# A four-layer fp32 transformer stack on one NeuronCore: a re-dealt beginning, sums held in PSUM, moved reciprocals and later weight pieces

## The chip, the cores and the metric

The kernel runs on one core of one Trainium2 chip. The metric is the device time of one execution in microseconds (us), here the median of several runs. A second kernel, the changed one, is compared with it run by run. The engines are named as the profile names them: PE is TensorE's matrix multiply, PEld its weight load, DVE is VectorE, ACT is ScalarE, POOL is GpSimd, and SP is SyncE, whose queue issues most DMA transfers. On-chip results of PE go to PSUM, which has eight banks; everything else is in SBUF.

## The reference

Four layers A, B, A, B with residual sums run over one sequence of 2048 tokens with 512 features, 32 heads of 16. Cut to what matters:

```python
def _A_ref(x, wqkv, w_phi, wo):              # 16 features per head, dual softmax
    q, k, v = split_heads(x @ wqkv)
    pq, pk = q @ w_phi, k @ w_phi            # per head
    phi_q = concat([softmax(pq), softmax(-pq)])
    phi_k = concat([softmax(pk), softmax(-pk)])
    kv, z = sum_s(phi_k * v), sum_s(phi_k)
    o = (phi_q @ kv) / (phi_q @ z + 1e-6)
    return o @ wo

def _B_ref(x, wq, wk, wv, wo, beta):         # 4 segments of 512 tokens
    for s in range(4):
        p = softmax(qs @ ks.T * 16 ** -0.5 + causal_mask)
        a_dot = p @ vs
        a_mem = (phi(qs) @ M) / (phi(qs) @ z + 1e-6)     # phi(t) = t + 1 or exp(t)
        o = g * a_mem + (1 - g) * a_dot                  # g = sigmoid(beta)
        M, z = M + phi(ks).T @ vs, z + sum(phi(ks))
    return o @ wo

x = x + A(layernorm(x)); x = x + B(layernorm(x))
x = x + A(layernorm(x)); x = x + B(layernorm(x))
```

The mask adds -1e9 where the query's index is below the key's, so a query here sees the keys up to its own. Inputs and output are float32, 2048 by 512.

## The kernel before

**Tiles.** A tile is 128 tokens by 512 features; a segment is four tiles (512 tokens). A product that must keep float32 accuracy is made from three products in the faster fp32r format: each operand is split into a high part (`hi`, a cast on ACT) and a low part (`lo`, the operand minus its high part, on DVE or POOL), and hi x hi, hi x lo and lo x hi are added in one PSUM bank. `mm3` issues these three for each of the four blocks of 128 input features (`kc` 0 to 3). PSUM is shared out as three banks named `g` for products of all kinds, one `pv`, one `mx`, one `my` and one pair `lg`.

**Order.** Every engine works its own instructions off in program order and waits by semaphores. The order in which the program issues them is written by hand. Several generators (projections of the next segment, output products of the last, weight pieces, layernorms) are advanced by tables of step names and numbers: a table entry says at which step which generator moves by how many pieces. So a table that changes shifts instructions on all engines at once.

**Layer A, first pass.** `LayerA.first` opens the program: `WARM` idle matmuls on zeros, then the transfers in the order of the string `ARRIVE` (x0 to x3 are the first four token tiles; k0, k1, v0, v1, q0, q1 the halves of the weights; `ident`, `bd`, `phi` small constants on ACT's queue), then the steps of the string `BEGINNING`. Its letters: m is a tile's statistics, g and r the root for a pair of tiles, n the normalisation, c the transposes of a tile with its split (`columns`), V, K, Q the split of one block of a weight matrix (a `p` behind it puts the low part on POOL), k and q a step of the fold, which multiplies phi into the key or query weights (transposes of the raw weights, then `phibd` matmuls), v a step of the value projection, u a step of the next segment's layernorm, p the spreading of phi. Later `pass1` projects all segments and sums the key-value products into `kva`. Near its end it fetches the output weights `awo`, high and low part of four blocks, eight pieces of 256 KB. They are advanced one piece at a step while t is 5 and 7 in a loop over the last eight projections. A transfer of that group is paced: it waits for the newest PE instruction at its place in the program.

**Layer A, second pass**, makes the numerators (the `KN` matmuls), divides, and multiplies by `awo` (`w` with `oh`, `ol`).

**Layer B** runs 32 half-head groups of four segments, each in five steps. In a step PE makes score products into `mx` and `my`, whose row maxima DVE takes (the custom instruction of the profile, with its accumulator `mxs`), then scores into `lg`, exponentials on ACT (`P`), the causal cut on POOL and the products with v into `pv`. The tables `GAPS` (segments before the last), `LAST`, `FINAL` (the last segment of the first and of the last layer B) and `BEFORE` say which filler moves in which step. When a pair of half-head groups is done, its denominators go through DRAM: `compact` loads them as `dn`, `flip` inverts them on DVE, `put` stores them, `load` fetches them spread over the heads into `KN` and `mmq`, and then `scaled`, `scaled_old` and `joined` use them on POOL. The offsets of these steps stand in `INVERT` and `JOIN`; the middle entry is for the two middle segments, the last for the last segment. Each is due so many steps after the group.

**The end of a layer B** (`close_last`) is written out in the string `TAIL`. There, p is the next piece of `early`, which multiplies the first three blocks of each of the last four token tiles by the output weights; P is all that is left of it; o transposes a tile of the last head group and divides it; t turns a tile back by a transpose, adds the memory's part and splits the sum; a multiplies the fourth block, adds the result to the tile `xe` (named `tb` in the profile) and stores it. `early` itself adds its partial sums to `xe` on DVE. In the first layer B steps of the next layer's projections stand between these; in the last layer nothing does.

The helpers through which all matmuls, transposes and other instructions are issued are lines 198, 202 and 176 of the profile, so groups are told apart by tile names.

Of the kernel before, what the change touches and what calls it, by code (L numbers as in the profile page):

```python
# [32 lines left out]
G = 3  # L33
# [77 lines left out]
3.0 x1 | 3.1 max | 3.3 pre out/2 | 3.4 out/2  # L111
4.1 max out/1~ | 4.3 pre out/3 x2 | 4.4 a3 out/1
5.1 max out/2 x3 | 5.3 fin out/2~ | 5.4 pre
6.1 max | 6.3 fin
7.1 pt p/2 | 7.3 p/4 fin | 7.4 p/3
"""
BEFORE = {-25: "q0 load", -23: "v0", -21: "k0", -18: "n", -17: "v1 n", -16: "n", -15: "n n", -14: "q1 n", -13: "n", -12: "k1 n", -11: "n", -10: "v2 n", -4: "max q2~", -1: "t0"}


@with_exitstack  # L120
def interleave_kernel(ctx, tc, x_in, a_wqkv, a_wphi, a_wo, b_wq, b_wk, b_wv, b_wo, b_beta,
# [504 lines left out]
    class LayerA:  # L626
# [88 lines left out]
        def pass1(self, first):  # L715
# [35 lines left out]
            for n, s in enumerate(SEGS):  # L751
# [121 lines left out]
                for t in range(8):  # L873
                    for n, _ in enumerate(kproj(t, e) if t < 4 else qproj(t - 4, e, later)):
                        if t == 7 and n == SEAM:
                            if QFIRST:
                                scale_q(e[5])
                            begun(2)
                            self.e.update({4 * s + t: e[4 + t] for t in range(3)})
                            seam()  # L880
                            self.second = self.pass2()
                            for _ in range(AHEAD):
                                next(self.second)
                        if t in (5, 7):
                            next(weights, None)
                        yield
# [114 lines left out]
    class LayerB:  # L1001
        def __init__(self, xsrc, xdst, cut, final):
            self.xsrc, self.xdst, self.cut, self.final = xsrc, xdst, cut, final
            self.st, self.hT, self.vv, self.ot, self.mx, self.U = {}, {}, {}, {}, {}, {}
            self.pr, self.pv, self.pk, self.num, self.old, self.oT = {}, {}, {}, {}, {}, {}
            self.dens, self.inv = {}, {}
            self.later, self.late, self.rows, self.xq = [], [], [], []
# [346 lines left out]
        def close_last(self, rest):  # L1354
# [16 lines left out]
            def turned(t):  # L1371
# [4 lines left out]
                act.copy(hi[:, cut], old[:, cut])  # L1376
                dve.tensor_tensor(out=lo[:, cut], in0=old[:, cut], in1=hi[:, cut].bitcast(F32), op=SUB)

            def added(t):
                po = PS("g", G)  # L1380
                for _ in self.product(po, s, t, range(NC - 1, NC)):
                    pass
                dve.tensor_tensor(out=self.xe[t], in0=po, in1=self.xe[t], op=ADD)
                sync.dma_start(out=self.xdst[4 * s + t], in_=self.xe[t])
# [9 lines left out]

        def product(self, po, s, t, kcs):
            yield from mm3(po, lambda a, kc: self.oT[s, kc][a][:, t * P : (t + 1) * P],
                           lambda b, kc: self.wo[b][:, kc, :], kcs)

# [17 lines left out]
        def early(self):  # L1416
# [229 lines left out]
```

## Time and profile before

| | us |
|---|---|
| median of 3 runs | 1425.59 |
| smallest and largest run | 1425.07 and 1429.27 |
| profiled execution, its own time | 1427.28 |
| span of the profiled execution | 1425.5 |
| PE busy in it | 1374.1 |
| DVE busy | 956.1 |
| ACT busy | 810.5 |
| POOL busy | 731.9 |
| HBM read and written | 115.54 MB and 41.55 MB |

How to read it: the span runs from the first to the last recorded instruction, and the profiled execution's own time is 1.8 us longer. A row of the timeline gives the start, the busy time, the engine, the line and operation, the tiles out<-in, the count, and in brackets the idle time before it on that engine with what ended it. A row of the windows gives the stretch, its length, the busy time of PE, PEld, DVE, ACT and POOL (with counts), the granted clock of PE as a share of full speed, the DMA engines' share and GB/s. A row of the waits gives who waited for whom: total us, times, and the longest. "issue" stands where an instruction waited for nothing that the profile shows.

### The profile page before, as it was taken

Reading aid. Unit: us, or ns where it says so; the run is one execution under the profiler, and the core shown is the slowest. Engines: PE = TensorE matmul, PEld = TensorE weight load, DVE = VectorE, ACT = ScalarE, POOL = GpSimd, SP = SyncE. Lnnn points to the kernel's source line nnn. Section 1 sums busy time; section 2 is a strip of 40 time slices with the busy share of each in tenths; the row PEclk is TensorE's granted clock in tenths of the full one; section 3 lists DMA queues with packets and bytes.
Section 4 is the critical chain, followed back from the end, with each engine's and each line's share of the span. In section 5 each row is a group of like instructions: output and inputs, shape, how many; then the busy total and the mean of one; then the engine's idle time right before and its main releaser. Section 6 shows DMA issues by size and latency. Waiting matters only on the chain.

```text
span 1425.5 us, 33178 instructions
## 1 busy us (share of the span) xinstructions
PE 1374.1 (96%) x12070; PEld 946.6 (66%) x12070; DVE 956.1 (67%) x3038; ACT 810.5 (57%) x1246; POOL 731.9 (51%) x1067
## 2 busy tenths in 40 slices
PE   9999999999999999999999999999999999999987
PEld 7787778765666565655568887886656565556544
DVE  5766788677667556667556768958776755666673
ACT  5555345447676566556544434553666755765654
POOL 1678765324565556544524446641455555654543
PEclk9999999999999999999999999999999999999999
DMA  5369275636655646556630104854465566555551
GB/s 196 119 226 335 93 253 174 188 112 181 185 138 159 174 119 176 153 164 188 195 132 33 60 31 132 269 179 142 127 185 151 140 182 159 143 162 145 141 141 68
DMA packets 134898, 222.72 MB, mean 156 GB/s; under 512 B 26032, under 2 KB 39472, under 8 KB 134736
## 3 DMA queue, kind: packets, MB, share of 16 engines
q1 hardware_dynamic: 132768, 219.96, 51.9%
q8 instruction: 97, 1.59, 0.5%
q10 hardware_dynamic: 1968, 0.64, 0.2%
q14 instruction: 65, 0.53, 0.1%
HBM read 115.54 MB, written 41.55 MB: 110 GB/s over the span
## 4 chain that ended last, share of the span: by engine, by line
PE 74%; DVE 8%; ACT 7%; DMA 4%; POOL 3%; issue 3%; SPq 1%; ACTq 0%; POOLq 0%; DVEq 0%
PE g L198 45%; PE pv L198 8%; PE lg L198 8%; PE mx L198 4%; PE g L202 3%; PE my L198 3%; ACT P L176 3%; POOL P L176 1%; PE lg L202 1%; DVE es L176 1%; DVE my L176 1%; DVE mx L176 1%; SPq L176 1%; DMA e<-ta 1%; DVE junk L176 1%
## 5 line engine op out<-in xcount | busy, mean ns | idle before, releaser
L176 ACT ACTIVATE P<-lg 128x1024 f32<-128x1024 f32 x316 | 325.0, 1028 | 176.2 <-PE lg L198 160.1
L176 POOL TENSOR_SCALAR_AFFINE_SELECT P<-P 128x256 f32<-128x256 f32 (+1 forms) x448 | 190.5, 440 | 406.7 <-ACT P L176 404.6
L176 DVE CUSTOM_DVE_ANT_0 junk<-mx,mask 128x128 uint8<-128x128 f32 (+2 forms) x384 | 147.3, 421 | 125.4 <-PE my L198 87.7
L198 PE MATMUL g<-hh,wqk 128*128 128x512 f32 x512 | 185.1, 410 | 0.7 <-ACT mt L176 0.7
L198 PE MATMUL lg<-e,e 64*128 64x512 f32 (+1 forms) x1010 | 166.1, 386 | 14.7 <-ACT P L176 13.7
L198 PE MATMUL g<-w,oh 128*128 128x512 f32 x512 | 171.0, 415 | 2.0 <-ACT oh L176 1.5
L198 PE MATMUL pv<-P,v 128*32 128x512 f32 (+3 forms) x2048 | 164.8, 439 | 5.3 <-ACT ot L176 5.3
L176 DVE CUSTOM_DVE_ANT_0 mx<-mx,mask 128x512 f32<-128x512 f32 x128 | 89.0, 695 | 107.1 <-PE my L198 84.7
L198 PEld LDWEIGHTS lg<-e,e 64*128 64x128 f32 x1010 | 80.0, 184 | 112.0 <-issue 50.4
L198 PE MATMUL my<-e,e 63*128 63x256 f32 (+3 forms) x519 | 147.8, 345 | 5.4 <-DVE mxs L176 4.2
L198 PE MATMUL mx<-e,e 63*128 63x256 f32 (+3 forms) x519 | 147.8, 336 | 0.8 <-DVE mxs L176 0.5
L176 DVE CUSTOM_DVE_ANT_0 junk<-my,mask 128x128 uint8<-128x128 f32 (+2 forms) x384 | 146.7, 419 | 0.0
L198 PE MATMUL g<-w,hh 128*128 128x512 f32 x448 | 143.8, 402 | 0.3 <-ACT hh L176 0.3
L198 PEld LDWEIGHTS pv<-P,v 128*32 128x32 f32 x2048 | 53.7, 109 | 106.9 <-issue 93.3
L198 PEld LDWEIGHTS g<-hh,wqk 128*128 128x128 f32 x512 | 96.2, 188 | 32.2 <-issue 11.8
L198 PEld LDWEIGHTS g<-w,oh 128*128 128x128 f32 x512 | 88.3, 189 | 32.5 <-issue 13.2
L198 PE MATMUL g<-w,ol 128*128 128x512 f32 x256 | 101.8, 398 | 3.7 <-DVE ol L176 3.1
L198 PE MATMUL g<-hl,wqk 128*128 128x512 f32 x256 | 100.3, 392 | 0.0
L176 DVE DVE_READ_ACCUMULATOR2_ANT mxs<- 128x1 f32 x1024 | 100.1, 98 | 0.0
L198 PEld LDWEIGHTS mx<-e,e 63*128 63x128 f32 (+1 forms) x519 | 90.5, 185 | 10.1 <-DVE mxs L176 4.2
L198 PEld LDWEIGHTS my<-e,e 63*128 63x128 f32 (+1 forms) x519 | 83.8, 185 | 17.7 <-DVE mxs L176 10.6
L198 PEld LDWEIGHTS g<-w,hh 128*128 128x128 f32 x448 | 80.3, 188 | 22.8 <-issue 6.3
(183 smaller groups left out, 2834.8 us busy)
## 6 DMA issues: line engine op xcount, KB each, us to landing
e<-ta SPq DMA_DIRECT2D x384, 128.0 KB
wqk<-wqk SPq DMA_DIRECT2D x64, 512.0 KB
x<-x SPq DMA_DIRECT2D x48, 256.0 KB
xr<-x SPq DMA_DIRECT2D x32, 256.0 KB
x<-xr SPq DMA_DIRECT2D x28, 256.0 KB
tmp<-U SPq DMA_DIRECT2D x56, 128.0 KB
KN<-inv SPq DMA_DIRECT2D x28, 256.0 KB
pq<-tb SPq DMA_DIRECT2D x24, 256.0 KB
```

Of the source, the lines that this page charges most:

```text
L176: i = f(*a, **k)
L198: return held(nc.tensor.matmul(*a, **k))
L202: return held(nc.tensor.transpose(*a))
```

## The change

It has six parts. (1) `ARRIVE`, `BEGINNING` and `WARM`: the key weights arrive ahead of the value weights and x2, x3 behind them, the fold of phi into the key weights runs ahead of the first token tile, tiles 2 and 3 get their statistics ahead of three low parts, and 12 idle matmuls take the place of 18. (2) `INVERT` and `JOIN`: for middle segments `flip` moves from offset 4.5 to 5.0 and `scaled_old` from 10.5 to 10.0; for the last segment `scaled` moves from 10.5 to 9.5. (3) The end of a layer B: `HELD` keeps the sums of tiles 2 and 3 in their PSUM bank, so that `added` goes on in it and `early` adds nothing on DVE; `BYPV` puts tile 1's last product in the `pv` bank; `LOWS` puts the low parts of tiles 0 to 2 on POOL; `TAIL` is written anew. `BYACT` is empty, so its branch is not used. (4) `AWO`: while t is 5 only two weight pieces are advanced in place of one at each step. (5) `UPC` moves one step from 14 to 13, which leaves every engine's order as it was. (6) Entries of `GAPS`, `LAST`, `FINAL` and `BEFORE` move by a step or a place.

```diff
-INVERT = (((2.5, 4.5, 5, 7), (2.5, 4.5, 5, 7), (2.5, 4.5, 5, 7), (2.5, 4.5, 5, 7)), ((2.5, 4.5, 5, 7), (2.5, 4.5, 5, 7), (2.5, 4.5, 5, 7), (2.5, 4.5, 5, 7)), ((2.5, 4.5, 5.5, 7.5), (2.5, 4.5, 5.5, 7.5), (2.5, 4.5, 5.5, 7.5), (2.5, 4.5, 5.5, 7.5)))
+INVERT = (((2.5, 4.5, 5, 7), (2.5, 4.5, 5, 7), (2.5, 4.5, 5, 7), (2.5, 4.5, 5, 7)), ((2.5, 5.0, 5, 7), (2.5, 5.0, 5, 7), (2.5, 5.0, 5, 7), (2.5, 5.0, 5, 7)), ((2.5, 4.5, 5.5, 7.5), (2.5, 4.5, 5.5, 7.5), (2.5, 4.5, 5.5, 7.5), (2.5, 4.5, 5.5, 7.5)))
...
-JOIN = (((9.5, None, None, 11, 12.5), (9.5, None, None, 11, 12.5), (9.5, None, None, 11, 12.5), (9.5, None, None, 11, 12.5)), ((9.5, 10.5, 11.5, 12, 13.5), (9.5, 10.5, 11.5, 12, 13.5), (9.5, 10.5, 11.5, 12, 13.5), (9.5, 10.5, 11.5, 12, 13.5)), ((10.5, 11.5, 12.5, 13, 13.5), (10.5, 11.5, 12.5, 13, 13.5), (10.5, 11.5, 12.5, 13, 13.5), (10.5, 11.5, 12.5, 13, 13.5)))
+JOIN = (((9.5, None, None, 11, 12.5), (9.5, None, None, 11, 12.5), (9.5, None, None, 11, 12.5), (9.5, None, None, 11, 12.5)), ((9.5, 10.0, 11.5, 12, 13.5), (9.5, 10.0, 11.5, 12, 13.5), (9.5, 10.0, 11.5, 12, 13.5), (9.5, 10.0, 11.5, 12, 13.5)), ((9.5, 11.5, 12.5, 13, 13.5), (9.5, 11.5, 12.5, 13, 13.5), (9.5, 11.5, 12.5, 13, 13.5), (9.5, 11.5, 12.5, 13, 13.5)))
...
-WARM = 18
+WARM = 12
 FEW = 2
-ARRIVE = "x0 ident x1 v0 bd v1 x2 x3 phi k0 k1 q0 q1"
+ARRIVE = "x0 x1 ident k0 bd phi k1 v0 v1 x2 x3 q0 q1"
 BEGINNING = """
-m0 m1 g0 r0 n0 V0 n1a V1p c0 V2 V3p c1 m2 m3 v1 v1 v1 v1 g1 r1 p n2 k k v1 n3a v1 v1 v1 c2 k k c3 u k v1 v1 v1 K0 K1 K2 K3 v1 u u q q u q u v1 q v1 v1 u u u q Q0 Q2 v1 Q1 u Q3 u u
+m0 m1 g0 r0 k k n0 n1a k c0 c1 k p V0 k V1p V2p m2 m3 g1 v1 r1 V3p v1 v1 n2 n3a v1 K0 c2 K1 K3 K2 v1 v1 c3 v1 u v1 v1 v1 q v1 q v1 u u u q u v1 q v1 v1 u u u v1 q Q0 Q2 u Q1 Q3 u u
 """
-TAIL = "p o0 p o1 o2 p p t0 p o3 p t1 t2 P a0 a1 t3 a2 a3"
+TAIL = "p o0 p o1 o2 t0 p p p p o3 t2 P t1 a0 t3 a1 a2 a3"
...
+BYPV = (1,)
+HELD = (2, 3)
+BYACT = ()
+LOWS = (0, 1, 2)
...
-UPC = (2, 3, 4, 5, 11, 12, 13, 14, 15)
+UPC = (2, 3, 4, 5, 11, 12, 13, 13, 15)
+AWO = 2
...
-6.1 k1+/3~ max | 6.2 m3 n | 6.3 out/3 | 6.4 a0+ out/1 v1+/2
-7.0 n | 7.1 max v1+/2 q2+/1 begin | 7.2 n | 7.3 q2+/3~ n N | 7.4 t0+ v2+/4 N
+6.1 k1+/3~ max | 6.2 m3 | 6.3 out/3 | 6.4 a0+ out/1 v1+/2
+7.0 n n | 7.1 max v1+/2 q2+/1 begin | 7.2 n | 7.3 q2+/3~ n N | 7.4 t0+ v2+/4 N
...
-2.1 max out/2 | 2.3 out/1 | 2.4 a2 x0 pre
+2.1 max out/1 | 2.3 out/2 | 2.4 a2 x0 pre
...
-4.1 max out/1~ | 4.3 pre out/3 x2 | 4.4 a3 out/1
-5.1 max out/2 x3 | 5.3 fin out/2~ | 5.4 pre
+4.1 max out/1~ | 4.3 pre out/2 x2 | 4.4 a3 out/2
+5.1 max out/2 x3 | 5.3 fin out/2 | 5.4 pre
...
-BEFORE = {-25: "q0 load", -23: "v0", -21: "k0", -18: "n", -17: "v1 n", -16: "n", -15: "n n", -14: "q1 n", -13: "n", -12: "k1 n", -11: "n", -10: "v2 n", -4: "max q2~", -1: "t0"}
+BEFORE = {-25: "q0 load", -23: "v0", -21: "k0", -18: "n", -17: "v1 n", -16: "n", -15: "n n", -14: "q1 n", -13: "n", -12: "k1 n n", -10: "v2 n", -4: "max q2~", -1: "t0"}
...
-    def mm3(po, lhs, rhs, kcs=range(NC)):
+    def mm3(po, lhs, rhs, kcs=range(NC), first=True, last=True):
 
         for kc in kcs:
             for n, (a, b) in enumerate(((0, 0), (0, 1), (1, 0))):
-                mm(po, lhsT=lhs(a, kc), rhs=rhs(b, kc), start=(kc == kcs[0] and n == 0),
-                   stop=(kc == kcs[-1] and n == 2))
+                mm(po, lhsT=lhs(a, kc), rhs=rhs(b, kc), start=(first and kc == kcs[0] and n == 0),
+                   stop=(last and kc == kcs[-1] and n == 2))
...
-                        if t in (5, 7):
+                        if t == 7 or t == 5 and n < AWO:
                             next(weights, None)
...
-                dve.tensor_tensor(out=lo[:, cut], in0=old[:, cut], in1=hi[:, cut].bitcast(F32), op=SUB)
+                (pool if t in LOWS else dve).tensor_tensor(out=lo[:, cut], in0=old[:, cut], in1=hi[:, cut].bitcast(F32), op=SUB)
 
             def added(t):
-                po = PS("g", G)
-                for _ in self.product(po, s, t, range(NC - 1, NC)):
+                held = self.held.pop(t, None)
+                po = held or (PS("pv", PV) if t in BYPV else PS("g", G))
+                for _ in self.product(po, s, t, range(NC - 1, NC), first=held is None):
                     pass
...
             for t in range(4):
                 po = PS("g", G)
+                if t in HELD:
+                    self.held[t] = po
+                    yield from self.product(po, s, t, EARLY, last=False)
+                    yield
+                    continue
                 yield from self.product(po, s, t, EARLY)
```

Three places show what this does to the order of instructions. The first is PE at the very start, before (`x` are token tiles, `w` the value weights' parts, `hh` and `hl` the parts of the transposed tokens):

```order
L198 MATMUL pv_147<-oh_145 128x512 x18
L202 MATMUL g_215<-ident,x_134 128x128 x4
L202 MATMUL g_226<-ident,x_135 128x128 x4
L198 MATMUL g_242<-w_182,hh_180 128x512
L198 MATMUL g_242<-w_183,hh_180 128x512
L198 MATMUL g_242<-w_182,hl_181 128x512
```

and in the change (`P` are the raw key weights, `e` their transposes):

```order
L203 MATMUL pv_147<-oh_145 128x512 x12
L207 MATMUL g_204<-ident,P_5_138 128x128 x4
L207 MATMUL g_210<-ident,P_5_138 128x128 x4
L207 MATMUL g_218<-ident,P_6_139 128x128 x4
L207 MATMUL g_224<-ident,x_134 128x128 x4
L207 MATMUL g_231<-ident,x_135 128x128 x4
L207 MATMUL g_238<-ident,P_6_139 128x128 x4
L203 MATMUL lg_250<-phibd,e_31_203 128x128 x8
L203 MATMUL mx_251<-phibd,e_31_203 128x128 x4
L203 MATMUL my_252<-phibd,e_31_203 128x128 x4
L203 MATMUL g_285<-w_176,hh_174 128x512
```

The key weights' transposes and the fold stand ahead of the first value product, where the token tiles' transposes and two tiles of value products stood.

The second is DVE in the middle segments of a layer B, before (ISA is the custom maximum and the reading of its accumulator; `dn` the denominators):

```order
L176 TENSOR_TENSOR hl_5787<-g_5894,hh_5786 128x4x128
L176 RECIPROCAL dn_5840<-dn_5840 128x64
L176 ISA mx_5915,mxs_5878<-mx_5915,mask 128x512
L176 ISA mxs_5878 128x1
L176 ISA my_5916,mxs_5878<-my_5916,mask 128x512
L176 TENSOR_TENSOR xr_5837<-g_5708,xr_5837 128x512
```

and in the change:

```order
L181 TENSOR_TENSOR hl_5781<-g_5888,hh_5780 128x4x128
L181 ISA mx_5908,mxs_5872<-mx_5908,mask 128x512
L181 ISA mxs_5872 128x1
L181 ISA my_5909,mxs_5872<-my_5909,mask 128x512
L181 RECIPROCAL dn_5834<-dn_5834 128x64
L181 TENSOR_TENSOR xr_5831<-g_5702,xr_5831 128x512
```

The reciprocal is behind the pair of maxima; it is so in sixteen places.

The third is DVE in the last rows of the last layer B, before (`tb` are the result tiles, `ot` the turned tiles, `ol` their low parts):

```order
L176 RECIPROCAL r_18381<-my_18351 128x4
L176 TENSOR_TENSOR tmp_18308<-my_18351,r_18381 128x64
L176 TENSOR_TENSOR ot_17957<-lg_18352,ot_17957 128x128
L176 TENSOR_TENSOR ol_18349<-ot_17957,oh_18348 128x128
L176 TENSOR_TENSOR tb_3509_17623<-g_18392,tb_3509_17623 128x512
L176 TENSOR_TENSOR tb_3547_17772<-g_18398,tb_3547_17772 128x512
L176 TENSOR_TENSOR ot_17957<-lg_18352,ot_17957 128x128
L176 TENSOR_TENSOR ol_18349<-ot_17957,oh_18348 128x128
L176 TENSOR_TENSOR tb_3579_17918<-g_18408,tb_3579_17918 128x512
L176 TENSOR_TENSOR tb_3626_18114<-g_18414,tb_3626_18114 128x512
```

and in the change:

```order
L181 RECIPROCAL r_18369<-my_18340 128x4
L181 TENSOR_TENSOR tmp_18298<-my_18340,r_18369 128x64
L181 TENSOR_TENSOR ot_17944<-lg_18341,ot_17944 128x128 x2
L181 TENSOR_TENSOR tb_3507_17613<-g_18380,tb_3507_17613 128x512
L181 TENSOR_TENSOR ot_17944<-lg_18341,ot_17944 128x128
L181 TENSOR_TENSOR ol_18338<-ot_17944,oh_18337 128x128
L181 TENSOR_TENSOR tb_3545_17762<-pv_18390,tb_3545_17762 128x512
L181 TENSOR_TENSOR tb_3577_17908<-g_18318,tb_3577_17908 128x512
L181 TENSOR_TENSOR tb_3624_18104<-g_18342,tb_3624_18104 128x512
```

One result add instead of two stands ahead of the last turned tile, and the low parts of the other three tiles are on POOL.

More of the change, by code (lines that the diff above doesn't have):

```diff
@@ L1005, in __init__ @@
             self.pr, self.pv, self.pk, self.num, self.old, self.oT = {}, {}, {}, {}, {}, {}
-            self.dens, self.inv = {}, {}
+            self.dens, self.inv, self.held = {}, {}, {}
             self.later, self.late, self.rows, self.xq = [], [], [], []
@@ L1376, in turned @@
                 act.copy(hi[:, cut], old[:, cut])
-                dve.tensor_tensor(out=lo[:, cut], in0=old[:, cut], in1=hi[:, cut].bitcast(F32), op=SUB)
+                (pool if t in LOWS else dve).tensor_tensor(out=lo[:, cut], in0=old[:, cut], in1=hi[:, cut].bitcast(F32), op=SUB)
             def added(t):
-                po = PS("g", G)
-                for _ in self.product(po, s, t, range(NC - 1, NC)):
-                    pass
-                dve.tensor_tensor(out=self.xe[t], in0=po, in1=self.xe[t], op=ADD)
+                held = self.held.pop(t, None)
+                po = held or (PS("pv", PV) if t in BYPV else PS("g", G))
+                for _ in self.product(po, s, t, range(NC - 1, NC), first=held is None):
+                    pass
+                if t in BYACT:
+                    mid = T2("tb3", 2)
+                    act.copy(mid, po)
+                    pool.tensor_tensor(out=self.xe[t], in0=mid, in1=self.xe[t], op=ADD)
+                else:
+                    dve.tensor_tensor(out=self.xe[t], in0=po, in1=self.xe[t], op=ADD)
                 sync.dma_start(out=self.xdst[4 * s + t], in_=self.xe[t])
@@ L1393, in close_last, with product @@
                     dict(o=own, t=turned, a=added)[what[0]](int(what[1]))
-        def product(self, po, s, t, kcs):
+        def product(self, po, s, t, kcs, first=True, last=True):
             yield from mm3(po, lambda a, kc: self.oT[s, kc][a][:, t * P : (t + 1) * P],
-                           lambda b, kc: self.wo[b][:, kc, :], kcs)
+                           lambda b, kc: self.wo[b][:, kc, :], kcs, first, last)
         def ask(self, s, t):
```

## The prediction, made before the changed kernel ran

> **What bounds the kernel now.** I read the page first, busy shares and then the chain that ended last, and after it the waits of PE alone, since the page leaves little doubt about the engine:
>
> ```profile
> PE 1374.1 (96%) x12070; PEld 946.6 (66%) x12070; DVE 956.1 (67%) x3038; ACT 810.5 (57%) x1246; POOL 731.9 (51%) x1067
> PE 74%; DVE 8%; ACT 7%; DMA 4%; POOL 3%; issue 3%; SPq 1%; ACTq 0%; POOLq 0%; DVEq 0%
> PE lg L198 <- ACT P L176: 13.7, 25, 1.1
> PE my L198 <- DVE mxs L176: 4.2, 18, 0.3
> PE my L198 <- issue: 2.1, 1, 2.1
> PE lg L202 <- DVE ot L176: 2.0, 3, 0.9
> ```
>
> PE is busy for 1374.1 of 1425.5 us, so only 51.4 us of idle PE time are there to be won, in many small pieces. The last four rows are groups of such pieces: total us, times, longest. The change does not take work from PE except idle matmuls at the very start, so each part can win only what it removes of these pieces. The three short chains without matmul cover, namely the beginning and the two ends of a layer B, I read instruction by instruction. All else I price by the PE gap that disappears.
>
> **Later weight pieces (first layer A, about 170 us).** The largest single gap is the one put down to "issue":
>
> ```profile
> 169.13 1.15 PE L198 MATMUL my<-P,v 128*32 128x32 f32 x110
> 172.42 0.38 PE L198 MATMUL my<-P,v 128*32 128x32 f32 x18 [2.15 <-issue]
> 178.40 1.17 PE L198 MATMUL g<-KN,P 128*64 128x68 f32 x32
> 869.15 1.29 PE L198 MATMUL my<-P,v 128*32 128x32 f32 x128
> 876.14 1.17 PE L198 MATMUL g<-KN,P 128*64 128x68 f32 x32
> 164.44 2.39 SPq L176 DMA_DIRECT2D w<-awo  x4
> q8 instruction: 1, 0.02, 15.5%
> 172.00:174.00 2.00, 1.58 (x22) 1.29 (x23) 1.57 (x5) 1.09 (x2) 1.13 (x2) 0.76 0.00 0
> 174.00:176.00 2.00, 2.00 (x8) 1.61 (x7) 0.58 (x2) 0.00 (x0) 2.00 (x2) 0.50 0.37 86
> ```
>
> PE stops in the midst of a run of 128 equal matmuls, with no data to wait for. The one instruction packet stands in the traffic view of 170.0 to 170.4 us, just behind the four `awo` pieces issued from 164.44 on; the same stretch of the second layer A runs without a stop. From the start of the run to the first `KN` matmul it takes 9.27 us here and 6.99 us there, so the stop and its clock cost 2.28 us. The clock is in the windows (first number after POOL's): 0.76, then 0.50. My reading: PE's next block of instructions queued behind 1 MB of weights. The change lets only two pieces go at that place, so the packet comes through some 3 us sooner and the boundary passes unseen: **-2.3**, bounds -2.3 and 0. The two last pieces of the weights are then issued late, and must be there before the fourth block of the first output tile (the second row below):
>
> ```profile
> 174.16 4.69 SPq L176 DMA_DIRECT2D w<-awo  x4
> 185.80 0.40 PE L198 MATMUL g<-w,oh 128*128 128x512 f32 x1
> 221.66 6.15 DMA xr<-in
> ```
>
> The last of them is issued near 178.85 now and some 0.9 us later in the change (one more issue of the four that take 4.69 us). It has about 6.0 us; the slowest landing of a 256 KB piece among the long pieces of the chain is 6.15 us, so at worst it is a little late. I cost it at nothing and keep +1 for two layers in the range.
>
> The Trainium skill, "Runtime: NRT & Kernel Launch", section "Instruction fetch mechanics", says instructions are refilled in 16 KiB blocks and that a crossing is mostly hidden by the issue rate; by it the stop would have another cause, the move of the weights would win nothing, and the sum would be 2.3 us smaller. The trace has one such packet of 0.02 MB right before a 2.15 us stop, so I give that rule the smaller chance.
>
> **The reciprocal behind the maxima (both layers B).** `flip` of the middle segments moves behind one pair of 512-wide maxima, sixteen times. It pays where VectorE had the maxima waiting:
>
> ```profile
> 441.40 0.54 DVE L176 RECIPROCAL dn<-dn 128x64 f32<-128x64 f32 x1
> 442.45 0.73 DVE L176 CUSTOM_DVE_ANT_0 my<-my,mask 128x512 f32<-128x512 f32 x1
> 443.30 0.38 PE L198 MATMUL my<-e,e 63*128 63x256 f32 x1 [0.27 <-DVE mxs L176]
> 557.84 0.38 PE L198 MATMUL my<-e,e 63*128 63x256 f32 x1 [0.26 <-DVE mxs L176]
> 470.15 0.55 DVE L176 RECIPROCAL dn<-dn 128x64 f32<-128x64 f32 x1
> 471.18 0.70 DVE L176 CUSTOM_DVE_ANT_0 mx<-mx,mask 128x512 f32<-128x512 f32 x1 [0.48 <-PE my L198]
> ```
>
> At 441 the order on VectorE is reciprocal, mx, my, and the two matmuls that reuse those banks start late; without the reciprocal ahead they could start about 0.5 us sooner. The same picture stands at 557.84 and at its two counterparts in the last layer, four places in all. At 470, and at the other places, VectorE waits for PE after the reciprocal (0.48 us here), so nothing is won. 4 x 0.5 = **-2.0**; bounds 0 (another wait takes over each time) and -2.2. The neighbouring shifts of `JOIN` are on POOL with slack and cost nothing. The price of the move is one more hold on SP's queue, priced in the third rival.
>
> **The end of each layer B: held sums, `TAIL`, low parts on POOL.** Two of the four tiles no longer add twice: their sums of the early products stay in PSUM. That takes two adds and three low-part subtractions off VectorE in each end. In the last end nothing else runs, so VectorE's queue is the path:
>
> ```profile
> 1417.48 0.33 PE L202 MATMUL lg<-ident,tmp 128*128 128x128 f32 x1 [0.88 <-DVE ot L176]
> 1418.86 1.28 DVE L176 TENSOR_TENSOR tb<-g,tb 128x512 f32<-128x512 f32 x2
> 1420.06 0.28 DVE L176 TENSOR_TENSOR ot<-lg,ot 128x128 f32<-128x128 f32 x1
> 1420.72 0.73 PE L198 MATMUL g<-w,oh 128*128 128x512 f32 x2 [0.70 <-ACT oh L176]
> 1420.91 1.51 DVE L176 TENSOR_TENSOR tb<-g,tb 128x512 f32<-128x512 f32 x2
> 739.34 0.72 PE L198 MATMUL g<-w,oh 128*128 128x512 f32 x2 [0.79 <-ACT oh L176]
> ```
>
> Now the fourth tile's `ot` add at 1420.06 stands behind two result adds (1.28 us), and the last add ends at 1420.91 + 1.51 = 1422.42. In the new order one add (0.7) stands ahead of the fourth tile; each transposed tile also starts sooner, because neither a low part nor an early add is queued ahead on VectorE. By hand I get: first transposed tile ready near 1415.5, fourth tile's `ot` ready 1418.1, its low part 1418.8, the four result adds one after another from 1417.2 with the last at 1420.6: **-1.8**. POOL's 128-wide subtraction has no row; the rows of that form on VectorE take 0.28 and a 512-wide one on POOL 1.48 (row in the next part). With three in a line at 1.48 the third ends near 1420.5 and the gain shrinks to almost nothing; I take the near end, as the tile is a quarter as wide. Bounds -2.2 and 0.
>
> The first end, near 740 us, has matmuls of the next layer as cover, and gaps like the 0.79 at 739.34 are all there is: **-0.5**, bounds -1.2 and +0.3 (two of the three `g` banks are held, and one product waits for the third).
>
> **Beginning.** The key weights now arrive ahead of the value weights, the fold of phi into them runs first, and 12 idle matmuls stand where 18 did:
>
> ```profile
> 1.36 6.45 PE L198 MATMUL pv<-oh 128*128 128x512 f32 x18 [1.36 <-POOL oh L176]
> 1.70 5.57 DMA P<-in
> 7.28 0.62 ACT L176 CAST w<-P 128x512 fp32r<-128x512 f32 x1 [1.06 <-DMA P<-in]
> 10.73 1.48 POOL L176 TENSOR_TENSOR w<-P,w 128x512 fp32r<-128x512 f32 x1 [0.23 <-ACT w L176]
> 18.30:22.30 4.00, 3.99 (x37) 3.99 (x37) 1.58 (x3) 1.79 (x4) 0.00 (x0) 1.00 0.61 190
> ```
>
> The third transfer lands at 7.27 whichever matrix it brings. PE then transposes two key blocks where it transposed x tiles at 8.05, so it starts some 0.8 us sooner; the fold that fills 18.8 to 22.5 moves to about 11 to 14.5. The first value product comes at 14.5 and waits about 0.5 us for POOL's low parts (1.48 each, and the third cannot start before ScalarE's third cast). From there the same matmuls follow. What is won at 7.3 is given back at the low parts and at one `g` bank: **0**, bounds -1.3 and +1.5. Twelve idle matmuls end near 1.36 + 12 x 0.36 = 5.7, with 1.6 us of silence after them; the stop at 170 shows that 2.15 us can halve the clock, which is inside the +1.5.
>
> The tables `GAPS`, `LAST`, `FINAL`, `BEFORE` shift output products by one or two places between neighbours that are PE work of the same kind; **0**, within 0.5 each way.
>
> **Sum.** -2.3 - 2.0 - 1.8 - 0.5 = -6.6 us. The profiled execution took 1427.28 us with a span of 1425.5 (1.8 around it), so it stands 1.7 above the median; the sum is a difference and I set it against the median: 1425.59 - 6.6 = **1419.0 us**. From one measurement to the next, 0.3% (4.3 us) is about what can be told from no change: below 1421.3 is faster, above 1429.9 slower.
>
> **Rivals.** First, *the stop stays*: the fetch still falls behind two weight pieces, or has another cause. Then -4.3, 1421.3, on the border. For it: 0.5 MB still goes ahead. Against: the second layer A. Second, *only the ends count*: the four maxima gaps are refilled by the next wait, PE <- ACT P being the largest group with 13.7 us. Then -2.3 - 1.2 (part of the tail) = -3.5, 1422.1; with the stop too, 1424.4: no change that can be told. Third, *SP is held longer*, the slower side:
>
> ```profile
> 442.35 0.55 SPq L176 DMA_DIRECT2D inv<-dn  x1
> 1335.26 0.44 SPq L176 DMA_DIRECT2D inv<-dn  x1
> 448.10 0.32 SPq L176 DMA_DIRECT2D wqk<-wqk  x1
> 615.11 5.22 DMA inv<-dn
> 628.25 0.56 PE L198 MATMUL lg<-e,e 64*128 64x256 f32 x4 [0.93 <-ACT P L176]
> ```
>
> `put` of the inverse can only go after the reciprocal; SP stands at it, and then at the load of its result, with six loads of the next scores behind. In the chain of waits the transfer at 615.11 takes 5.22 us and the scores behind it cost PE 0.93 at 628.25. Setting the new end of each reciprocal (after its maxima) against the old `put`, eleven of the sixteen (the first at 442.35, the last at 1335.26) are later, by 0.4 to 2.5 us, 19 us in sum. If half of that reaches PE, +9.7 stands against the -2.0: -6.6 + 2.0 + 9.7 = +5.1, 1430.7. It decides from the point at which the hold outlasts the slack in front of SP's next work: at 442.35 that is large (the next load behind the pair is at 448.10), and only near 641 and 1335 do the loads follow at once. So I hold it for unlikely. Fourth, *the change's parts work, but code and transfers shift* so that a new stop of 2.3 us appears elsewhere or the weights land late twice (+1): 1420 to 1421.3.
>
> **How the numbers follow.** Forecast with all four terms, within 2 us of 1419: 0.47. Stop stays, or a new one: 0.20 (1421.3, half of it on either side of the border). Only the ends count: 0.20. Held SP: 0.08 (slower by over 0.3% in most of it), other late transfers 0.05 (no change). Faster 0.47 + 0.10 + 0.06 = 0.63; slower 0.08; no change 0.29. The range goes from all bounds good, -2.3 - 2.2 - 2.2 - 1.2 - 1.3 = -9.2 (1416.4, with 1.9 more for the tables and the median's spread: 1414.5), to 1427, which leaves out the held SP; the likeliest case by itself is 1416.5 to 1421.5.
>
> **What would show it.** Stop: no wait on "issue" near 170, 7.0 us from the run of 128 to the first `KN`, granted clock 1.00 there. Reciprocal: PE <- DVE mxs falls from 4.2 to about 3, and no new gap behind `lg` near 645 or 1340. End: the fourth tile's `ot` add ahead of three of the four result adds, and no gap like the 0.70 before the last products. Beginning: the first value products near 15 and the second tile's values as early as now, about 22. Wrong would be a larger PE <- ACT P after `put`, POOL's small subtractions at over 1 us, or a clock below 1.00 before 12 us.

## The result, and the profile after

| | us |
|---|---|
| before, median of 20 runs | 1425.77 (1423.69 to 1431.53) |
| changed, median of 20 runs | 1420.41 (1416.06 to 1427.37) |
| changed to before | 0.9958, 95% interval 0.9946 to 0.9969 |
| span of the profiled execution, before and changed | 1425.5 and 1419.1 |

The change makes the kernel 0.42% faster, between 0.31% and 0.54%: some 6 us by this ratio, 5.4 us between the two medians. The forecast was 1419.0 us, that is 6.6 us less. First come the page's busy shares and chain of the changed kernel, then its waits of PE (total us, times, longest):

```profile
PE 1372.4 (97%) x12064; PEld 945.4 (67%) x12064; DVE 953.2 (67%) x3027; ACT 810.1 (57%) x1246; POOL 735.4 (52%) x1074
PE 72%; DVE 8%; ACT 6%; POOL 5%; DMA 5%; issue 3%; SPq 1%; ACTq 0%; DVEq 0%; POOLq 0%
PE lg L203 <- ACT P L181: 11.2, 22, 1.1
PE my L203 <- DVE mxs L181: 3.2, 14, 0.3
PE g L207 <- DMA P<-in: 1.2, 2, 0.9
PE lg L207 <- DVE ot L181: 1.0, 2, 0.6
PE g L203 <- POOL w L181: 0.8, 1, 0.8
PE my L203 <- issue: 0.7, 2, 0.4
```

PE is still the bound. Of the waits shown before, "issue" fell from 2.1 to 0.7, mxs from 4.2 to 3.2, ACT P from 13.7 to 11.2 and `ot` from 2.0 to 1.0. New are the waits on `P<-in` and on POOL's `w`, both in the beginning.

Now to the places of the prediction, one by one. Near 170 us, PE's timeline of the changed kernel and one window behind it:

```profile
169.56 1.20 PE L203 MATMUL my<-P,v 128*32 128x32 f32 x116
170.96 0.32 PE L203 MATMUL my<-P,v 128*32 128x32 f32 x12 [0.20 <-issue]
176.54 1.17 PE L203 MATMUL g<-KN,P 128*64 128x68 f32 x32
172.00:174.00 2.00, 1.27 (x6) 0.57 (x4) 1.58 (x5) 1.52 (x2) 0.98 (x1) 1.00 0.32 76
```

The stop is 0.20 in place of 2.15, the clock stays at 1.00, and from the run to the first `KN` it takes 6.98 us, the 7.0 that was named. In the middle of a layer B, VectorE and PE now show:

```profile
439.31 0.69 DVE L181 CUSTOM_DVE_ANT_0 mx<-mx,mask 128x512 f32<-128x512 f32 x1
440.57 0.55 DVE L181 RECIPROCAL dn<-dn 128x64 f32<-128x64 f32 x1
440.76 0.38 PE L203 MATMUL my<-e,e 63*128 63x256 f32 x1
```

The reciprocal stands behind the maxima, and the matmul has no bracket: it follows without a gap where 0.27 us stood. The last end, on PE, DVE and POOL:

```profile
1407.16 0.64 PE L203 MATMUL pv<-P,v 128*32 128x256 f32 x8
1413.11 0.28 DVE L181 TENSOR_TENSOR ot<-lg,ot 128x128 f32<-128x128 f32 x1
1413.96 0.68 DVE L181 TENSOR_TENSOR tb<-pv,tb 128x512 f32<-128x512 f32 x1
1414.56 1.28 DVE L181 TENSOR_TENSOR tb<-g,tb 128x512 f32<-128x512 f32 x2
1411.07 0.46 POOL L181 TENSOR_TENSOR ol<-ot,oh 128x128 fp32r<-128x128 f32 x1 [5.30 <-ACT oh L181]
```

The fourth tile's `ot` at 1413.11 has three of the four result adds behind it. From the end of the last attention product (1407.80) to the end of the last add (1415.84) it is 8.04 us; before, a product ending at 1412.67 and an add ending at 1422.42 made 9.75.

### The profile page after: what moved, and what is told of

Same layout as the page of the kernel before. It is cut to its first block, busy times and chain, and to the rows that moved or that the text cites. A ratio compares the mean times of both kernels' runs of the same rounds, so it can differ in the third digit from the quotient of the medians.

```text
span 1419.1 us, 33156 instructions
## 1 busy us (share of the span) xinstructions
PE 1372.4 (97%) x12064; PEld 945.4 (67%) x12064; DVE 953.2 (67%) x3027; ACT 810.1 (57%) x1246; POOL 735.4 (52%) x1074
## 4 chain that ended last, share of the span: by engine, by line
PE 72%; DVE 8%; ACT 6%; POOL 5%; DMA 5%; issue 3%; SPq 1%; ACTq 0%; DVEq 0%; POOLq 0%
PE g L203 44%; PE pv L203 8%; PE lg L203 8%; PE mx L203 4%; PE g L207 3%; ACT P L181 3%; DMA e<-ta 3%; PE my L203 3%; POOL P L181 2%; PE lg L207 2%; DVE es L181 1%; POOL tb L181 1%; POOL tmp L181 1%; DVE junk L181 1%; SPq L181 1%
## 5 line engine op out<-in xcount | busy, mean ns | idle before, releaser
L203 PE MATMUL lg<-e,e 64*128 64x512 f32 (+1 forms) x1010 | 166.3, 387 | 12.0 <-ACT P L181 11.2
L203 PEld LDWEIGHTS mx<-e,e 63*128 63x128 f32 (+1 forms) x519 | 90.8, 186 | 10.4 <-DVE mxs L181 4.3
```

Of the source, the lines that this page charges most:

```text
L203: return held(nc.tensor.matmul(*a, **k))
```

## The experiments

All ran beside the kernel before. Since one execution differs from the next by some us, timed ratios settle only what is larger than about 0.15% (2 us). So I also cut the profiled executions at the same matmuls of the program (counted within their kind), which gives the time of the same stretch of work in each, and compared these stretches. Every kernel whose part in a stretch is unchanged is a further sample of it; this gives 14 profiles.

**One part alone, four kernels.** Each is the kernel before with one part of the change:

```diff
 e1_awo:   +AWO = 2
 e2_flip:  middle INVERT  -(2.5, 4.5, 5, 7)  +(2.5, 5.0, 5, 7)
 e3_end:   new TAIL, +BYPV = (1,)  +HELD = (2, 3)  +LOWS = (0, 1, 2)
 e4_begin: new ARRIVE and BEGINNING, -WARM = 18  +WARM = 12
```

> The kernel before with AWO = 2 alone: two weight pieces instead of four while t is 5. Theory (PE's instruction packet queued behind the weights): the 2.15 us stop on issue near 170 us is gone or under 0.3 us, 9.27 us from the run of 128 to the first KN matmul becomes about 7.0, time -2.3 us against before. Rival (the stop has another cause that a later part of the change removed, such as the shorter start of PE's stream): stop stays near 2 us, time 0.

> The kernel before with the middle entry of INVERT alone (flip 4.5 to 5.0). Theory: the 0.27 us waits on mxs at 443, 557, 1140 and 1254 vanish, about 0.5 us each, -2.0 us; the last segment untouched. Rival A (SP is held longer): new PE waits on ACT P behind the put, time 0 to +5. Rival B (the middle segments gain more than the four gaps, as the profile after suggests with 4.0 and 3.0 us in the two layers, and flip is its cause): -5 to -7 before the last segment, part of it given back there.

> The kernel before with TAIL, HELD, BYPV and LOWS alone. Theory: last end -1.8 us, first end -0.5 us, together -2.3 us. Rival (POOL's small subtractions are slow, over 1 us each, and hold the last products): -0.5 to 0.

> The kernel before with ARRIVE, BEGINNING and WARM alone. Theory: gained at 7.3 us and given back at POOL's low part, 0 us within -0.3 and +0.8 (the profile after has PE 0.4 us later at 53 us). Rival (shorter warming slows the first products): clock under 1.00 before 12 us, +1.5 us or more.

| | median us | to before | interval |
|---|---|---|---|
| e1_awo | 1426.48 | 1.0002 | 0.9991 to 1.0013 |
| e2_flip | 1424.27 | 0.9990 | 0.9977 to 1.0002 |
| e3_end | 1425.92 | 0.9991 | 0.9980 to 1.0001 |
| e4_begin | 1427.91 | 1.0006 | 0.9992 to 1.0020 |

None of the four is told from no change by its time; the interval of e1_awo, which goes down to -1.3 us, leaves out the -2.3 us that its theory named. The profiles say more. The stop on issue near 170 us, in PE's timeline of e1_awo, e3_end and e4_begin in this order:

```profile
171.02 0.38 PE L203 MATMUL my<-P,v 128*32 128x32 f32 x18 [0.50 <-issue]
172.38 0.38 PE L203 MATMUL my<-P,v 128*32 128x32 f32 x18 [1.87 <-issue]
173.49 0.32 PE L203 MATMUL my<-P,v 128*32 128x32 f32 x12 [1.57 <-issue]
```

With two pieces it is short, with four long. But in e3_end and e4_begin, where it is long, the stretch from the first layer A's beginning (46 us) to its end (245 us) takes 196.4 and 196.1 us, against 195.8 in e1_awo and 198.9 in the kernel before: the stops of 1.87 and 1.57 us cost 0.6 and 0.3 us, the one of 2.15 us cost 3 us. What sets them apart is taken up below, under the weight pieces.

In e2_flip PE's waits of `my` on mxs are 3.1 us in all against 3.9 to 4.7 in the kernels without it, but the stretches of the middle segments are 233.6 and 232.4, within the spread of the unchanged ones (232.9 to 234.8, and 231.8 to 233.3). Shorter stretches show the effect without that spread. These are the `mxs` transposes around the first of the four places, in the kernel before and in e2_flip:

```profile
438.96 0.28 PE L202 MATMUL g<-ident,mxs 128*16 128x128 f32 x1
452.11 0.28 PE L202 MATMUL g<-ident,mxs 128*16 128x128 f32 x1
436.73 0.28 PE L207 MATMUL g<-ident,mxs 128*16 128x128 f32 x1
449.44 0.28 PE L207 MATMUL g<-ident,mxs 128*16 128x128 f32 x1
```

From one to the next it is 13.15 us and 12.71. At all four places it is 13.09 to 13.19 us in the five profiles with the old order and 12.64 to 12.75 in all nine with the new one, so `flip` alone wins some 0.44 us at each, 1.8 in all. Rival B, the larger gain, does not show. Rival A does, at one place of the last layer: ScalarE stands 2.91 us behind the loads of the next scores, which are queued on SP behind `put` and `load`, and PE waits for ScalarE:

```profile
1343.60 1.02 ACT L181 ACTIVATE P<-lg 128x1024 f32<-128x1024 f32 x1 [2.91 <-DMA e<-ta]
1344.68 0.56 PE L203 MATMUL lg<-e,e 64*128 64x256 f32 x4 [0.95 <-ACT P L181]
```

The last end of e3_end:

```profile
1412.54 0.64 PE L203 MATMUL pv<-P,v 128*32 128x256 f32 x8
1419.95 1.28 DVE L181 TENSOR_TENSOR tb<-g,tb 128x512 f32<-128x512 f32 x2
```

From 1413.18 to 1421.23 it is 8.05 us: the end alone brings its 1.7. In e4_begin the rival's clock shows: PE stands 2.05 us before the first transposes, the clock is 0.50 from 8 to 10 us, and the second tile's key products, at 45.7 us in the kernel before, start at 47.0. Its timed runs (+0.9 us, between -1.1 and +2.9) decide nothing between theory and rival.

**The rest of the change, and two parts undone.** The first two are the kernel before with a part, the last two the changed kernel with one part taken back:

```diff
 e5_join:     new INVERT and JOIN
 e6_tables:   new GAPS, LAST, FINAL, BEFORE, UPC
 e7_scaled:   last JOIN  -(9.5, 11.5, 12.5, 13, 13.5)  +(10.5, 11.5, 12.5, 13, 13.5)
 e8_oldbegin: old ARRIVE, BEGINNING, -WARM = 12  +WARM = 18
```

> The kernel before with all of INVERT and JOIN. The flip alone won about 0.5 us in each layer B's middle segments, where the changed kernel wins some 2.5 and 1.7 against the mean of unchanged profiles. Theory (scaled_old half a step sooner on POOL frees the causal cuts behind it): middle segments (from 426 to 661 us of the profile before) 231.2 us as in the changed kernel, 231.0 in the last layer, time -3 to -4 us against before. Rival (the tables did it, by taking a layernorm piece out of step 6.2): middle segments 233.5 and 232.4, time -1 us or less.

> The kernel before with GAPS, LAST, FINAL, BEFORE and UPC alone. Theory (JOIN does it): middle segments 233.5 and 232.7 us as in the unchanged ones, time within 1 us of before. Rival (the tables do it): middle segments 231.5 and 231.3, time -3 us.

> The changed kernel with scaled of the last segment back at 10.5. In the changed kernel PE stands 1.49 us at 681 us behind ACT's ot, where five other profiles show 0.50, and half clock follows. Theory (POOL waits at scaled for the load of the inverse, with the causal cuts behind it): 0.50 there, full clock to 688 us, time 1 to 2 us under the changed kernel. Rival (PE only comes sooner to a transfer that is not sooner): 1.5 us again, time equal to the changed kernel's within 1 us.

> The changed kernel with ARRIVE, BEGINNING and WARM of before. Theory (the new beginning costs 0.4 to 1.3 us): the second tile's key products at 46 us start at 45.7 instead of 46.2 to 47.0, time 0.5 to 1 us under the changed kernel. Rival (the beginning is neutral, what differs is when the transfers land): equal within 0.3 us.

| | median us | to before | interval | middle segments, first and last layer B, us |
|---|---|---|---|---|
| e5_join | 1425.94 | 0.9991 | 0.9975 to 1.0007 | 231.1 and 233.4 |
| e6_tables | 1426.14 | 0.9997 | 0.9981 to 1.0013 | 233.2 and 232.0 |
| e7_scaled | 1419.15 | 0.9955 | 0.9938 to 0.9971 | 232.9 and 231.2 |
| e8_oldbegin | 1421.57 | 0.9962 | 0.9947 to 0.9977 | 232.4 and 231.4 |

e5_join won in the first layer what was expected, and nothing in the last, where 231.0 us was named; its time is 1.3 us below before (between -3.6 and +1.0), not 3 to 4. e6_tables is as expected of a part that does nothing. So the tables alone are not what shortens the middle segments. With the tables alone the last end takes 10.4 us (a product ending at 1409.17, and the last add below), more than 9.75; with the new end they cost nothing (8.05 in e3_end without them, 8.04 in the changed kernel with them).

```profile
1418.90 0.69 DVE L181 TENSOR_TENSOR tb<-g,tb 128x512 f32<-128x512 f32 x1 [0.24 <-PE g L203]
```

The question for e7_scaled was the last segment of the first layer B. In the profile after, two of its rows and a window show where part of the gain is given back:

```profile
680.97 1.29 PE L203 MATMUL pv<-P,v 128*32 128x512 f32 x16 [1.49 <-ACT ot L181]
688.53 0.46 PE L203 MATMUL mx<-e,e 63*128 63x512 f32 x1 [0.49 <-DVE mxs L181]
684.00:686.00 2.00, 2.00 (x7) 1.51 (x6) 0.00 (x0) 0.92 (x2) 1.60 (x3) 0.50 1.03 264
```

A gap of 1.49, then half clock. In e7_scaled the gap is 0.51 and the clock stays full there, as its theory said; its time (0.9955) is equal to the changed kernel's, as its rival said. Two later kernels with the early `scaled` show 0.50 and 0.51 too, e8_oldbegin 1.12. Between the `mxs` transposes around this place (673 to 689 us of the profile before) it takes 17.3 us in the changed kernel and 16.5 in e8_oldbegin, and 15.9 in all other twelve. So the early `scaled` can cost 0.6 to 1.4 us there, in two of five profiles, and no profile without it lost them; over the whole segment (661 to 707 us) that is lost in the spread, 46.2 to 50.0 us with it and 45.9 to 50.3 without.

e8_oldbegin has its key products at 45.7 us, as its theory said, but its time (0.9962) is not below the changed kernel's (0.9958); the two intervals cover each other's value, so neither theory nor rival is decided.

**Four more of the changed kernel.**

```diff
 e9_nolows:     -LOWS = (0, 1, 2)  +LOWS = ()
 e10_warm18:    as e7_scaled, and -WARM = 12  +WARM = 18
 e11_noawo:     four weight pieces while t is 5
 e12_oldbegin2: as e7_scaled, with the old beginning of e8_oldbegin
```

> The changed kernel with LOWS empty: the low parts of the last three turned tiles back on VectorE. From the end of the last attention product to the end of the last result add every profile with the old end has 9.74 us, every one with the new end 8.05. Theory (held sums and the order of TAIL carry the gain, POOL's share is small): 8.4 to 8.8. Rival (POOL carries it): 9.4 or more.

> The changed kernel with scaled of the last segment at 10.5 and WARM 18. Three profiles with the new beginning stand 0.91, 1.24 and 2.05 us before the first key transposes; in the last two the clock is 0.50 for some 2 us from 8 to 12 us, and the second tile's key products come at 47.5 and 47.0 instead of 46.2. Theory (12 idle matmuls end too early): clock 1.00 from 6 us on, key products at 46.0 to 46.3, time 0.5 to 1 us under the run with scaled at 10.5 and WARM 12. Rival (the clock falls whatever precedes, or six more matmuls hold up the first transposes): 46.8 or later.

> The changed kernel with all four weight pieces back while t is 5. Six profiles with four pieces stop 1.3 to 2.15 us on issue at 170 us, four with two pieces 0.2 to 0.8. Theory (the pieces set the stop, and the clock after it costs more in some executions): stop over 1.2 us, first layer A's stretch from 46 to 242 us 196.0 to 199 instead of 195.8, time 0.5 to 2.5 us over the changed kernel. Rival (the rest of the change moved the boundary): stop under 0.8 us, time equal.

> The changed kernel with the old beginning (ARRIVE, BEGINNING, WARM) and scaled of the last segment at 10.5. Theory (the beginning costs 0.4 to 1.8 us, the early scaled up to 1): key products at 45.7, PE waits about 0.5 us on ACT's ot near 681 us, the fastest of all, 1418 to 1419 us on a chip where before has 1426. Rival (neither matters beyond the spread from execution to execution): equal to the changed kernel within 1 us.

| | median us | to before | interval |
|---|---|---|---|
| e9_nolows | 1420.60 | 0.9948 | 0.9927 to 0.9968 |
| e10_warm18 | 1421.47 | 0.9954 | 0.9939 to 0.9969 |
| e11_noawo | 1420.84 | 0.9953 | 0.9933 to 0.9974 |
| e12_oldbegin2 | 1420.65 | 0.9945 | 0.9925 to 0.9964 |

e9_nolows: the last end takes 8.84 us, so POOL's share is 0.8 of the 1.7 and the held sums and the new order have 0.9; the theory had POOL's share smaller. e11_noawo: the stop is back (1.02 near 174 us, and 1.30 in the second layer A near 868), so the pieces set it. But it is shorter than the 1.2 us that was named, and the first stretch takes 195.9 as with two pieces; only the second is longer, 242.0 against 240.7 to 241.4, and the time (0.9953) is no longer than that of the changed kernel. e12_oldbegin2 has 45.8 us for the beginning and a gap of 0.50 before 679 us, as expected; it has the lowest ratio of all, 0.9945, but its interval reaches past the changed kernel's 0.9958, so it isn't shown to be a better version.

e10_warm18 missed what its theory named. The windows of its beginning, then of e11_noawo's (12 idle matmuls), with the gap ahead in e11_noawo:

```profile
8.00:10.00 2.00, 2.00 (x19) 1.81 (x17) 0.67 (x2) 1.03 (x3) 0.10 (x1) 1.00 1.04 384
20.00:24.00 4.00, 3.81 (x15) 3.21 (x16) 2.69 (x6) 3.31 (x7) 0.00 (x0) 0.61 0.22 70
```

```profile
7.88 2.79 PE L207 MATMUL g<-ident,P 128*128 128x128 f32 x12 [2.19 <-DMA P<-in]
8.00:10.00 2.00, 2.00 (x10) 2.00 (x11) 0.08 (x1) 0.72 (x2) 0.17 (x1) 0.50 1.04 371
20.00:24.00 4.00, 3.64 (x14) 2.77 (x14) 2.69 (x5) 3.73 (x7) 0.00 (x0) 0.66 0.21 69
```

With 18 idle matmuls there is no gap before the first transposes and the clock stays at 1.00 there. But it falls to 0.61 after 20 us, behind the second soft place of the new beginning, and the key products come at 48.2 us, which is in the rival's range. That place stands in the profile after as two rows:

```profile
18.55 0.50 PE L203 MATMUL g<-w,hh 128*128 128x512 f32 x1 [0.84 <-POOL w L181]
19.64 0.63 PE L207 MATMUL g<-ident,x 128*128 128x128 f32 x4 [0.36 <-DVE x L181]
```

## Why the prediction was right, point by point

The stretches, as means over the profiles without and with the part (number of profiles, smallest to largest), beside the term of the sum:

| stretch, by the profile before | without, us | with, us | difference | term |
|---|---|---|---|---|
| beginning, 0 to 46 | 45.7 (8, 45.4 to 45.8) | 47.2 (5, 46.2 to 48.7) | +1.5 | 0 |
| first layer A, 46 to 245 | 196.8 (7, 195.8 to 198.9) | 195.8 (7, 195.7 to 196.0) | -0.9 | -2.3 |
| second layer A, 741 to 981 | 241.5 (7, 240.6 to 243.2) | 240.9 (7, 240.7 to 241.4) | -0.65 | 0 |
| middle segments, first layer B, 426 to 661 | 233.7 (5, 232.9 to 234.8) | 232.0 (8, 231.0 to 234.1) | -1.7 | -1.0 |
| middle segments, last layer B, 1123 to 1356 | 232.6 (5, 231.8 to 233.3) | 231.4 (8, 230.4 to 233.4) | -1.1 | -1.0 |
| end of the first layer B, 707 to 741 | 33.79 (6, 33.74 to 33.81) | 33.17 (8, 33.13 to 33.29) | -0.6 | -0.5 |
| last end, last product to last add | 9.74 (5, 9.73 to 9.76) | 8.05 (7, 8.04 to 8.06) | -1.7 | -1.8 |

"With" for the beginning is the new one with 12 idle matmuls; for the middle segments it is INVERT and JOIN together, and e2_flip, which has only the first, is in neither column. The differences sum to -5.2 us; the forecast's terms were -6.6, the timed difference of the medians is -5.4. That the total came so near is luck in part: the beginning cost 1.5 us that was put at nothing, the weight pieces brought 0.7 less, and the middle segments 0.8 more for a reason that the prediction did not have.

**The bound and the ends** were right, in place and in size. The two ends repeat within 0.16 us in all profiles; these chains can be counted by hand. POOL's small subtraction, which had no row, took 0.46 us.

**The reciprocal** was right in its mechanism and nearly in its size. The four places bring some 0.44 us each where 0.5 was taken, 1.8 in all, in every one of the nine profiles with it, e2_flip among them. In the middle segments of one layer PE's waits on mxs sum to 0.80 to 1.16 us in the profiles without it and to 0.26 to 0.77 with it. The stretches win 2.8 with `JOIN`, which the prediction put at nothing. Where the other 1.0 comes from is open: it is no larger than the spread between executions, and the waits on ACT P in these segments are only some 0.3 us shorter on average (3.4 to 3.1 in the first layer, about 3.0 in the last either way). The third rival, SP held at `put`, showed at one place, and it is the one that the prediction had named, near 1340: PE waits 0.95 us there in e2_flip, 1.04 in e5_join, 0.40 in e12_oldbegin2, and the profile shows no gap in the other six with the late `flip`, nor in the five with the old one. With the late `flip` the load of the inverse goes 5.4 us ahead of the `mxs` transpose at 1340, in e2_flip as in the changed kernel, against 7.3 in e6_tables with the old order. That slack is lost in each of them, but in the changed kernel's own profile PE doesn't wait; what the rival priced at 9.7 us came to at most 1.

**The weight pieces** were right in the mechanism and wrong in size. In seven profiles with four pieces the stop in the first layer A is 1.0 to 2.15 us; in seven with two it is 0.2 to 0.8. That PE stops for its instructions, the traces of all fourteen bear out. The stop falls behind 110 of the 128 matmuls in the nine kernels with 18 idle matmuls and behind 116 in the five with 12, hence at the same count of PE's instructions from the start; and a packet of 16 KB on the profile's instruction queue q8 starts 2.2 to 2.7 us before PE goes on, each time. With two pieces this packet starts 0.4 to 1.3 us ahead of the run of 128, with four between 0.2 ahead and 1.0 behind its start; on average it comes 1.3 us sooner with two, where the prediction had some 3.

The failing step is the one that took the 9.27 against 6.99 us of one profiled execution for the cost. Measured in the same way, over both layers A of all fourteen profiles:

| stop, us | from the run to the first `KN`, us | half clock behind it |
|---|---|---|
| none, or up to 0.8 | 6.95 to 7.01 | no |
| 1.02, 1.30, 1.32 | 6.98, 7.04, 7.00 | no |
| 1.57, 1.60 | 7.09, 7.11 | no |
| 1.87, 1.91 | 7.40, 7.42 | no |
| 2.15, 2.15, 2.17 | 9.27, 9.26, 9.24 | yes |

```profile
169.25 1.15 PE L203 MATMUL my<-P,v 128*32 128x32 f32 x110
171.72 0.38 PE L203 MATMUL my<-P,v 128*32 128x32 f32 x18 [1.32 <-issue]
176.26 1.17 PE L203 MATMUL g<-KN,P 128*64 128x68 f32 x32
173.04:176.45 3.41, 3.41 (x12) 2.79 (x11) 1.99 (x4) 0.05 (x1) 2.69 (x3) 0.50 0.28 64
```

The three rows are e2_flip's, where a stop of 1.32 us costs nothing, and the window is the half clock of the kernel before. Up to some 1.3 us a stop only takes the place of other waits: in e12_oldbegin2, with a stop of 0.23, PE waits 0.47 us for VectorE's `kva` and 0.37 for POOL's `P` ahead of `KN`, and in e2_flip neither wait is there. Only the three longest stops drew the half clock, 3.41 us at 0.50, and these account for about two thirds of the gain. The profile that the prediction was made from held one of them. The second layer A, which I read as running without a stop, has one of 1.3 to 2.2 in three of the seven (1.91 in e3_end, 2.17 in e5_join, 1.30 in e11_noawo), and its stretch is longer in these (241.8, 243.2 and 242.0 us), though e4_begin has 241.5 without a stop. Together the pieces bring 1.6 us on average over the stretches, 1.1 from the run to `KN` alone. The timed runs of e1_awo and e11_noawo show no gain; e1_awo's interval (-1.3 to +1.9 us) leaves out the 1.6 and not the 1.1, e11_noawo's leaves out neither. No late weights appeared.

**The beginning** was wrong by +1.5, the upper bound I had given. The step that failed is "what is won at 7.3 is given back", with no price for the clock. The first key transposes don't start at 7.3 but at 7.75 to 8.13, since PE now stands at the transfer itself, and 12 idle matmuls leave 0.9 to 2.2 us of silence before. In three of the five profiles with 12, and in none of the eight with the old beginning, the clock then halves, before 12 us: a sign of being wrong that the prediction had named, though the changed kernel's own profile doesn't have it. In the two whose clock held the key products come 0.5 and 0.8 us later than with the old beginning, in the three others 1.3, 1.8 and 3.0. The wait for POOL's third low part is 0.84 where I took 0.5, with another 0.36 behind it. Whether that costs the timed runs as much stays open: the changed kernel and e7_scaled have 0.9958 and 0.9955, the same two with the old beginning 0.9962 and 0.9945.

**The tables** cost and bring nothing that can be told (0.9997), as forecast, though they lengthen the old end and not the new one.

**What the parts sum to** is open as well. e1_awo, e3_end, e4_begin, e5_join and e6_tables deviate by +0.02, -0.09, +0.06, -0.09 and -0.03%, -0.13% in sum, while the whole change brings -0.42%. The half widths of the six intervals, added as squares, are about 0.33%, so the 0.29% between may be chance, or the parts may help each other; the profiles of the ends are the only place where I saw the latter.

## What to carry to other kernels

A chain with no cover can be priced from a single profile to a tenth or two of a us, as the two ends were. A gap in the midst of busy work cannot: here a stop of up to 1.3 us only took the place of other waits, and the clock fell behind it in some executions and not in others. Take several profiles, or other kernels with the same stretch, before putting a number on such a gap, and look at the granted clock behind it. A part that makes PE wait for a transfer itself, in place of work that was waiting behind other work, has to be charged for the clock too.

## What the runs showed of the hardware

Gaps of PE well under 3 us can halve the granted clock. All six gaps between 2.05 and 2.19 us in the fourteen profiles did so. A shorter gap does so in one execution and not in another: before the transposes near 1390 us PE stands 1.13 to 1.24 us in all fourteen, and half clock begins within 2.2 us behind it in three (e3_end, e4_begin and e12_oldbegin2; in the first two with a shorter gap in between). In e12_oldbegin2 and e9_nolows the gap is the same:

```profile
1390.44 0.66 PE L207 MATMUL g<-ident,U 128*128 128x128 f32 x4 [1.24 <-ACT U L181]
1391.89:1395.30 3.41, 3.41 (x22) 0.97 (x25) 0.00 (x0) 1.74 (x3) 3.41 (x5) 0.50 0.22 77
1390.47 0.65 PE L207 MATMUL g<-ident,U 128*128 128x128 f32 x4 [1.24 <-ACT U L181]
1391.89:1395.30 3.41, 3.41 (x39) 1.52 (x40) 0.00 (x0) 1.80 (x4) 3.41 (x5) 1.00 0.23 77
```

In e9_nolows PE also stands 1.83 us before the first transposes and keeps its clock, while e11_noawo above lost it after 2.19:

```profile
8.13 1.06 PE L207 MATMUL g<-ident,P 128*128 128x128 f32 x8 [1.83 <-DMA P<-in]
8.00:10.00 2.00, 1.53 (x12) 1.32 (x13) 0.01 (x1) 1.21 (x3) 0.00 (x0) 1.00 1.05 404
```

e7_scaled lost it after 1.24, with another gap of 0.47 close behind. The pair of 0.84 and 0.36 near 19 us halved it in e10_warm18 and e11_noawo only, out of six profiles with that pair. Every stretch of half clock that ends before the kernel does is 3.41 us long in these profiles, so one costs at most 1.7 us. The Trainium skill, "TensorE: Matmul & The Clock Gate", section "HAM oscillation — how this bites in real kernels", gives as a rule that PE should have no gap above about 3.4 us; here gaps of a third of that were enough, so the measurement decides. The same page of the Trainium skill, section "Part 1: The HAM clock gate (the "warmup" mystery)", says that the window of 3413 ns runs freely; the 3.41 us agree with it, and so does a gap that costs in some executions only.

The other surprise is the stop on issue itself: with nothing changed ahead of it, it was between 1.3 and 2.15 us near 170 us in five profiled executions (before, e2_flip, e3_end, e5_join, e6_tables), and it came in the second layer A in some and not in others.
